# A third sum of g taken by accumulating DMAs in 7 of 25 blocks, with g stored by token halves and the steps from block 8 on in another order

## The chip, the cores and the metric

The kernel runs on one core of one Trainium2 chip. A core has a matrix engine (TensorE, PE in the profile), a vector engine (VectorE, DVE), a scalar engine (ScalarE, ACT), GpSimd (POOL), a queue engine (SyncE, SP) and 16 DMA engines which all queues share. PE reads its operands from on-chip memory and writes into the accumulation memory (PSUM); DVE and ACT read and write both; a DMA can't reach PSUM. Every engine works through its own instruction list in order and waits on semaphores for the others.

The metric is the device time of one execution in microseconds (us). The times of the kernel before are 685.28, 685.20 and 685.03 us, median 685.2.

## The reference

An attention over channels, followed by a feed-forward layer with a tanh-GELU. All inputs are float32.

```python
# q, k, v: (4, 6080, 256); w_in: (256, 2048); w_out: (2048, 256)
qn = q / (norm(q, axis=1) + 1e-6)
kn = k / (norm(k, axis=1) + 1e-6)
s = kn.transpose(0, 2, 1) @ qn / tau          # (4, 256, 256)
a = softmax(s, axis=-1)
x = (v @ a).reshape(24320, 256)
h = x @ w_in
g = 0.5 * h * (1 + tanh(c * (h + 0.044715 * h**3)))
out = g @ w_out                               # (24320, 256)
```

## The kernel before

**The stages.** For each of the four batches the kernel loads q and k as bfloat16, forms their 256x256 product (`gram_row`), the column norms and the softmax, and multiplies the result into the first weight, so that `aw` = a·w_in (256x2048) stands ready for the batch. After that h is `aw` applied to v, and no x is ever formed. This preparation for batch b+1 is spread among the steps of batch b; in the last batch there is none left to spread.

**The blocks.** The tokens are cut into 25 blocks: five of 1024 and one of 960 in each of the first three batches (blocks 0 to 17), five of 1024, one of 512 and one of 448 in the last (blocks 18 to 24). In a block v arrives twice transposed: `lv` issues a casting DMA from POOL into a DRAM buffer (`cast_v`), and `lt` a transposing DMA from SP into `vT` (`load_vt`).

**The first product** makes h with d_ff on the partitions, 16 chunks of 128 by the tokens of the block. Some chunks are computed plainly (`plain`, words `g.`, and `plain_gelu`, words `G.`). The others go in pairs, one chunk of the lower half of d_ff and one of the upper, by a Strassen-Winograd scheme with seven products instead of eight (`small`, words `m1` to `m7`, and `set_step`, words `wcq`, `wy5`, `wap`, `wax`, and the GELUs `wGq`, `wGr`, `wGx`). The GELUs are ACT's and write g as bfloat16 into two tiles for each block, `g_half(n, f)`, where f is the half of d_ff. A tile is `[128, 8, tokens]`: chunk by chunk, with all tokens of the block behind each other.

**The second product** is the same scheme on g: d_ff is cut in two (f = 0, 1), the tokens are cut in two (t = 0, 1), and the output channels are cut in two. Writing g_ft for a quarter of g, DVE forms four sums of quarters in `token_sum` (words `T1` to `T4`, line 704, each in two parts h = 0, 1 of four chunks, that is 128 x 2048 elements in a 1024-token block):

```
T1 = g01 - g00     T2 = g11 - T1     T3 = g11 - g01 (written over g01)     T4 = g10 - T2
```

`product` (line 708; words `M1` to `M7`) then runs four matmuls for each part: M1, M2 and M3 take g00, g10 and g11 into the accumulator `r`; M5, M6, M7 and M4 take T1, T2, T3 and T4 into the accumulator `p`. So T3.h is read by M7.h alone, and M7 is the product whose line reads `p<-g,wcomb` in the profile, since T3 lies in a g tile. The weights for it, with the sums S1 to S4 of quarters of w_out, are built once by `prep_wout` at line 662. `mm2_step` (line 761) combines the accumulators and transposes the results out of them (`c11`, `c12`, `c21`, `c22`), and SP stores them. The last block multiplies directly (`direct`, words `D`).

**The order.** The whole program after the first batch's preparation is one string `ORDER` (line 948) of 3,498 words, such as `T3.0:18` (T3, part 0, block 18) or `m1.2@a:19` (in PSUM bank a). `run` (line 874) takes them one by one, and each puts its instructions at the end of its engine's list. So this string fixes the order on every engine, and that of the DMAs on POOL and SP too. A word stands about where its step is to start: PE's words between two others tell how much matmul work lies between them.

Of the kernel before, what the change touches and what calls it, by code (L numbers as in the profile page):

```python
# [16 lines left out]
def kernel(  # L17
# [493 lines left out]
    def plain_gelu(n, u):  # L511
        t = BLOCKS[n][2]
        hc = t // 2
        hp = PR.pop((n, u))
        if t > 512:
            nc.scalar.activation(g_half(n, u // 8)[:, u % 8].rearrange("p (t x) -> p t x", t=2),  # L516
                                 hp[:, :, :hc], AF.Gelu_apprx_tanh)
        else:
            nc.scalar.activation(g_half(n, u // 4)[:, u % 4 * 2 : u % 4 * 2 + 2, :], hp[:, :, :t],
                                 AF.Gelu_apprx_tanh)  # L520
# [13 lines left out]
    def half_gelu(n, p, t):  # L534
        hc = hc_of(n)
        nc.scalar.activation(g_half(n, p // 4)[:, p % 4 * 2 : p % 4 * 2 + 2, t * hc : t * hc + hc],
                             PR.pop((n, p, t))[:, :, :hc], AF.Gelu_apprx_tanh)
# [69 lines left out]
    def set_step(n, i, what):  # L607
# [54 lines left out]
    def prep_wout(what):  # L662
        if what == "pA11":
            nc.vector.tensor_copy(wc(A11), w_half(0, 0))
        if what == "pF0":
            WF.append(yout.tile([128, 32, 32], FP32, tag="ot", name="wf0"))
            nc.vector.tensor_add(WF[0], w_half(1, 0), w_half(1, 1))
        if what == "pS1":
            nc.vector.tensor_copy(wc(S1), WF[0])
        if what == "pF1":  # L670
            WF.append(yout.tile([128, 32, 32], FP32, tag="ot", name="wf1"))
            nc.vector.tensor_sub(WF[1], WF[0], w_half(0, 0))
# [10 lines left out]
        if what == "pS3":  # L683
            nc.vector.tensor_sub(wc(S3), w_half(0, 0), w_half(1, 0))
# [3 lines left out]
    def quarter(n, f, t, h):  # L688
        hc = hc_of(n)
        return GT[n, f][:, h * 4 : h * 4 + 4, t * hc : t * hc + hc]  # L690

    def token_sum(n, i, h):
# [11 lines left out]
        nc.vector.tensor_sub(o, a, b)  # L704
# [20 lines left out]
    def direct(n, p, t, tag):  # L725

        hc = hc_of(n)
        for m in range(2):
# [218 lines left out]

ORDER = """
# [84 lines left out]
ap:6 sa.2:2 wap.5:7 M7.1:6 T4.1:6 m3.5:7 m7.5:7 M3.0:6 ksq.3:2 wGx.2:7 qsq.3:2 G.4:7 M3.1:6 m1.6@a:7  # L1033
wGq.5:7 f1.3:2 wax.5:7 M7.0:6 m5.6@h:7 m4.5:7 m5.7@b:7 wcq.6:7 c12:6 wy5.6:7 m1.7@r:7 ax:6 m6.6:7
wcq.7:7 M4.0:6 m6.7:7 lq.6:2 lk.6:2 f2.3:2 wGr.5:7 wap.6:7 wy5.7:7 m7.6:7 f3.3:2 wGx.5:7 wap.7:7
m2.6:7 m3.6:7 wax.6:7 M4.1:6 m2.7:7 m7.7:7 c21:6 wGq.6:7 wGx.6:7 wax.7:7 row.3_5@p:2 row.2_4@p:2
m3.7:7 row.3_1@p:2 row.3_2@p:2 row.2_0@p:2 m1.1@s:8 T1.0:7 m4.7:7 wGq.7:7 row.2_5@p:2 m4.6:7 wGx.7:7
row.3_3@p:2 g.8@h:8 vs:8 row.2_2@p:2 row.3_4@p:2 m5.1@b:8 row.3_0@p:2 wGr.6:7 wcq.1:8 sp.3@a:2
row.2_1@p:2 G.8:8 lv.0:10 wy5.1:8 wGr.7:7 m6.1:8 row.2_3@p:2 g.12@h:7 m2.1:8 T1.1:7 wap.1:8 sa.3:2
ksq.4:2 m3.1:8 qsq.4:2 m7.1:8 M5.1@r:7 lv.1:10 M5.0@r:7 m1.2@a:8 wax.1:8 T2.0:7 gc:2 f1.4:2 wGq.1:8  # L1040
G.12:7 m5.2@b:8 m4.1:8 T4.0:7 f2.4:2 wcq.2:8 wy5.2:8 g.0@h:8 wGr.1:8 G.0:8 M1.0@p:7 m6.2:8 m2.2:8
M1.1@p:7 y5:7 g.3@h:8 lt.0:9 lt.1:9 cq:7 wap.2:8 wGx.1:8 f3.4:2 c22:6 sp.4@s:2 sa.4:2 G.3:8 T2.1:7
m3.2:8 M2.1:7 m1.5@s:8 M2.0:7 M6.1:7 m5.5@h:8 wGq.2:8 m7.2:8 lq.7:2 wcq.5:8 T3.0:7 qsq.5:2 T3.1:7
ksq.5:2 wy5.5:8 M6.0:7 m2.5:8 g.11@b:8 m6.5:8 c11:7 wax.2:8 ap:7 f1.5:2 wap.5:8 m4.2:8 G.11:8
wGx.2:8 wGr.2:8 M3.0:7 M3.1:7 f2.5:2 m3.5:8 f3.5:2 wGq.5:8 c12:7 m5.6@b:8 m1.6@a:8 m7.5:8 lk.7:2
M7.1:7 wy5.6:8 sp.5@p:2 M7.0:7 wcq.6:8 qsq.6:2 wax.5:8 T4.1:7 sa.5:2 ax:7 m2.6:8 m4.5:8 m6.6:8
g.4@h:8 row.5_5@p:2 wap.6:8 ksq.6:2 M4.0:7 wGx.5:8 wGr.5:8 m3.6:8 f1.6:2 row.5_4@p:2 row.5_3@p:2
m1.7@s:8 row.4_0@p:2 G.4:8 m7.6:8 m5.7@h:8 row.4_5@p:2 wcq.7:8 wy5.7:8 row.4_2@p:2 m6.7:8 T1.0:8
wax.6:8 wap.7:8 f2.6:2 wGq.6:8 wGx.6:8 row.5_0@p:2 M4.1:7 m2.7:8 c21:7 m7.7:8 m3.7:8 g.12@b:8
wGq.7:8 wax.7:8 row.4_4@p:2 m4.7:8 m4.6:8 f3.6:2 row.4_3@p:2 sp.6@r:2 G.12:8 wGr.6:8 wGr.7:8 T1.1:8  # L1050
g.0@h:9 row.5_2@p:2 row.5_1@p:2 m1.1@a:9 sa.6:2 vs:9 row.4_1@p:2 M5.1@r:8 m5.1@b:9 m1.2@s:9 M5.0@r:8
wGx.7:8 wcq.1:9 gc:2 qsq.7:2 G.0:9 c22:7 M1.1@p:8 wy5.1:9 y5:8 T2.1:8 m6.1:9 wap.1:9 M1.0@p:8
m5.2@h:9 wcq.2:9 cq:8 m2.1:9 m6.2:9 m3.1:9 lv.0:11 m7.1:9 T2.0:8 M2.0:8 M6.0:8 wy5.2:9 wap.2:9
wax.1:9 T3.0:8 m3.2:9 wGq.1:9 ksq.7:2 f1.7:2 wGx.1:9 m4.1:9 wGr.1:9 M2.1:8 m7.2:9 m2.2:9 M6.1:8
m1.3@a:9 wax.2:9 f2.7:2 m5.3@b:9 m4.2:9 c11:8 f3.7:2 ap:8 wGq.2:9 g.8@h:9 wcq.3:9 m6.3:9 wGr.2:9
# [18 lines left out]
m7.6:10 m1.7@r:10 wGq.6:10 wax.6:10 m5.7@b:10 wcq.7:10 wy5.7:10 g.0@h:11 G.0:11 c12:9 m6.7:10
wap.7:10 eT:2 wGx.6:10 m4.6:10 M4.0:9 m2.7:10 m7.7:10 m3.7:10 rsum@a:2 M4.1:9 T1.0:10 g.4@h:11
wax.7:10 m4.7:10 rs:2 c21:9 wGr.6:10 wGq.7:10 aw.0@p:2 aw.1@a:2 m1.1@s:11 G.4:11 vs:11 m5.1@b:11
wGr.7:10 wcq.1:11 g.8@h:11 m6.1:11 wy5.1:11 T1.1:10 M5.0@r:10 ac.1:2 wGx.7:10 wap.1:11 ac.0:2
lt.0:12 M5.1@r:10 c22:9 m7.1:11 wax.1:11 m1.2@a:11 aw.4@p:2 G.8:11 m3.1:11 m5.2@h:11 wcq.2:11 ac.4:2
# [202 lines left out]
```

## Time and profile before

| | value |
|---|---|
| median of 3 runs | 685.2 us (685.03 to 685.28) |
| the profiled execution | 685.17 us, of which 683.4 us are the span that the profile shows |
| granted PE clock | 0.998 of full |
| ACT busy | 621.7 us, 91% |
| POOL busy | 74.1 us, 11% |
| DVE, the sums at line 704 with 2048 elements a partition | 160 of about 1.21 us, and 24 of 1.14 us with 1920 |
| DVE, T3 alone in 1024-token blocks | 40 of 1.211 us |
| DMA share by 16 engines, mean | 67% (software-issued 35.3%, SP's 31.4%) |

How to read the profile: busy time is the union of an engine's instructions. A matmul's record runs from its start to its modelled end, and matmuls overlap in the pipeline; the step from one start to the next tells the rate, the record's length does not. "Idle before" is the time for which the engine stood still before the instructions of a group, with what released it. A line `x4` in a timeline is four instructions merged. The "idle" of POOL's DMA issues is no loss in itself: they wait on purpose for a point in PE's list.

### The profile page before, as it was taken

Reading aid. Unit: us, or ns where it says so; the run is one execution under the profiler, and the core shown is the slowest. Engines: PE = TensorE matmul, PEld = TensorE weight load, DVE = VectorE, ACT = ScalarE, POOL = GpSimd, SP = SyncE. Lnnn points to the kernel's source line nnn. Section 1 sums busy time; section 2 is a strip of 40 time slices with the busy share of each in tenths; the row PEclk is TensorE's granted clock in tenths of the full one; section 3 lists DMA queues with packets and bytes.
Section 4 is the critical chain, followed back from the end, with each engine's and each line's share of the span. In section 5 each row is a group of like instructions: output and inputs, shape, how many; then the busy total and the mean of one; then the engine's idle time right before and its main releaser. Section 6 shows DMA issues by size and latency. Waiting matters only on the chain.

```text
span 683.4 us, 10285 instructions
## 1 busy us (share of the span) xinstructions
PE 665.6 (97%) x3585; PEld 337.1 (49%) x3585; DVE 628.5 (92%) x938; ACT 621.7 (91%) x941; POOL 74.1 (11%) x137
## 2 busy tenths in 40 slices
PE   3999999999999999999999999999999999999997
PEld 2854545454445454444444545545444444444566
DVE  4569999999999999989999999999999999999994
ACT  5389999998899999999989999999988999999983
POOL 4322111011001111010010011101000000000001
PEclk9999999999999999999999999999999999999999
DMA  9998988694677795646467977657275336534415
GB/s 240 208 248 142 160 153 136 106 150 76 120 131 113 134 167 88 108 69 114 85 107 123 178 124 133 104 81 122 43 112 78 48 63 103 85 71 91 76 32 90
DMA packets 161508, 78.80 MB, mean 115 GB/s; under 512 B 148512, under 2 KB 152224, under 8 KB 160736
## 3 DMA queue, kind: packets, MB, share of 16 engines
q0 software_dynamic: 14480, 39.72, 35.3%
q1 hardware_dynamic: 145728, 37.14, 31.4%
q10 hardware_dynamic: 1248, 1.28, 0.6%
q8 instruction: 28, 0.46, 0.3%
q14 instruction: 24, 0.20, 0.1%
HBM read 78.91 MB, written 36.57 MB: 169 GB/s over the span
## 4 chain that ended last, share of the span: by engine, by line
PE 94%; DMA 4%; DVE 0%; ACT 0%; issue 0%; POOL 0%; DVEq 0%; ACTq 0%; POOLq 0%
PE p L482 24%; PE r L482 18%; PE rb L482 17%; PE qp L482 13%; PE h L482 12%; PE G L205 5%; DMA qk_g1b<-in_k_dram 3%; PE e L482 2%; PE awp L374 2%; DMA qk_g1a<-in_q_dram 1%; PE o L482 1%; PE ss L186 0%; PE ss L263 0%; ACT qp L613 0%; PE rk L317 0%
## 5 line engine op out<-in xcount | busy, mean ns | idle before, releaser
L482 PEld LDWEIGHTS <-wcomb 128*128 128x128 bf16 x1408 | 136.6, 98 | 144.5 <-issue 1.3
L482 PE MATMUL p<-t,wcomb 128*128 128x512 bf16 (+2 forms) x576 | 142.5, 373 | 0.0
L482 PE MATMUL r<-g,wcomb 128*128 128x512 bf16 (+2 forms) x576 | 141.7, 373 | 0.0
L626 ACT ACTIVATE g<-qp 128x1024 bf16<-128x1024 f32 (+1 forms) x130 | 132.5, 1023 | 4.4 <-PE qp L482 4.1
L482 PEld LDWEIGHTS <-aw 128*128 128x128 bf16 x872 | 84.7, 98 | 91.3 <-DVE aw L416 1.3
L704 DVE TENSOR_TENSOR t<-g,t 128x2048 bf16<-128x2048 bf16 (+2 forms) x96 | 112.9, 1183 | 0.0
L482 PE MATMUL rb<-tv,sw 128*128 128x512 bf16 (+3 forms) x288 | 100.1, 366 | 0.5 <-ACT qp L613 0.3
L618 DVE TENSOR_TENSOR qp<-rb,yw 128x512 f32<-128x512 f32 (+2 forms) x137 | 93.4, 686 | 7.5 <-ACT yw L616 4.0
L621 DVE TENSOR_TENSOR xw<-rb,yw 128x512 f32<-128x512 f32 (+2 forms) x137 | 92.3, 677 | 5.3 <-PE rb L482 3.8
L516 ACT ACTIVATE g<-h 128x1024 bf16<-128x1024 f32 (+1 forms) x92 | 94.2, 1031 | 2.4 <-PE h L482 2.4
L482 PE MATMUL h<-vT,aw 128*128 128x512 bf16 (+2 forms) x376 | 94.4, 377 | 0.0
L613 ACT ACTIVATE qp<-rb 128x512 f32<-128x512 f32 (+2 forms) x137 | 81.0, 596 | 7.5 <-PE rb L482 5.6
L616 ACT ACTIVATE yw<-qp 128x512 f32<-128x512 f32 (+2 forms) x137 | 81.2, 599 | 5.6 <-PE qp L482 4.2
L482 PEld LDWEIGHTS <-sw 128*128 128x128 bf16 x576 | 56.1, 98 | 56.4 <-issue 1.8
L637 ACT ACTIVATE g<-xw 128x512 bf16<-128x512 f32 (+1 forms) x130 | 82.3, 636 | 0.8 <-DVE xw L621 0.6
L637 ACT ACTIVATE g<-rb 128x512 bf16<-128x512 f32 (+1 forms) x130 | 77.8, 604 | 2.6 <-PE rb L482 2.2
L442 POOL DMA_DIRECT2D vb<-in_v_dram x45 | 22.5, 500 | 338.8 <-PE rb L482 172.2
L704 DVE TENSOR_TENSOR t<-g 128x2048 bf16<-128x2048 bf16 (+2 forms) x48 | 56.7, 1183 | 0.2
L704 DVE TENSOR_TENSOR g<-g,g 128x2048 bf16<-128x2048 bf16 (+2 forms) x48 | 56.6, 1181 | 0.0
L482 PE MATMUL qp<-vT,sw 128*128 128x512 bf16 (+3 forms) x144 | 51.4, 366 | 0.0
L482 PE MATMUL rb<-vT,aw 128*128 128x512 bf16 (+3 forms) x144 | 51.1, 366 | 0.0
L482 PE MATMUL rb<-tv,aw 128*128 128x512 bf16 (+3 forms) x144 | 51.0, 366 | 0.0
(145 smaller groups left out, 816.0 us busy)
## 6 DMA issues: line engine op xcount, KB each, us to landing
out_dram<-ot SPq DMA_DIRECT2D x160, 128.0 KB, 3.0
vb<-in_v_dram POOLq DMA_DIRECT2D x38, 256.0 KB, 4.2
k<-in_k_dram POOLq DMA_DIRECT2D x21, 384.0 KB, 5.4
q<-in_q_dram POOLq DMA_DIRECT2D x21, 384.0 KB, 4.7
out_dram<-ot SPq DMA_DIRECT2D x24, 120.0 KB, 3.0
wst<-in_moe_w_out_dram POOLq DMA_DIRECT2D x2, 1024.0 KB, 11.2
vb<-in_v_dram POOLq DMA_DIRECT2D x6, 240.0 KB, 4.0
qk_f<-in_k_dram ACTq DMA_DIRECT2D x2, 512.0 KB, 7.2
```

The source lines that it names most:

```text
L205: nc.tensor.matmul(G[b][:, jc, :], lhsT=qt[:np_, r, jc * 128 : jc * 128 + 128], rhs=kt[:np_, r, :], start=first and jc == 0, stop=jc == 1, ...
L374: nc.tensor.matmul(ps, lhsT=ET[b][:, jc, ic * 128 : ic * 128 + 128], rhs=win_bf[:, jc, fs * 512 : fs * 512 + 512], start=jc == 0, stop=jc ...
L442: after(nc.gpsimd.dma_start(out=vb[: y - x, :], in_=v[b, t0 + x : t0 + y, :]), gate)
L482: GATE[0] = nc.tensor.matmul(*a, skip_group_check=True, **kw)
L516: nc.scalar.activation(g_half(n, u // 8)[:, u % 8].rearrange("p (t x) -> p t x", t=2), hp[:, :, :hc], AF.Gelu_apprx_tanh)
L613: apart(n, i, 0, "act", nc.scalar.activation(QP[n, i][:, 0, :w], RB[n, i][:, :w], AF.Copy))
L616: apart(n, i, 1, "act", nc.scalar.activation(YW[n, i][:, :w], QP[n, i][:, 1, :w], AF.Copy))
L618: apart(n, i, 1, "dve", nc.vector.tensor_add(QP[n, i][:, 1, :w], RB[n, i][:, :w], YW[n, i][:, :w]))
L621: nc.vector.tensor_add(XW[n, i][:, :w], RB[n, i][:, :w], YW.pop((n, i))[:, :w])
L626: nc.scalar.activation(g[:, k0].rearrange("p (t x) -> p t x", t=2), qp[:, :, :hc], AF.Gelu_apprx_tanh)
L637: nc.scalar.activation(g[:, k0, t], x[:, :w], AF.Gelu_apprx_tanh)
L704: nc.vector.tensor_sub(o, a, b)
```

## The change

Five edits:

1. g is stored by token halves: the tile is `[128, 2, 8, tokens/2]` and no longer `[128, 8, tokens]`, so a quarter's part of four chunks is one contiguous run of 4 KB in each partition. All GELU writes and all reads of g follow.
2. The signs of the second product change, so that T3 is a sum: T1 = g01 - g00, T2 = g11 + T1, T3 = g11 + g01, T4 = g10 - T2, with S1, S2 and S3 of w_out negated to match (`pF0`, `pF1`, `pS3`).
3. In blocks 8, 9, 18, 19, 20, 21 and 22 T3 is not DVE's: POOL issues a DMA that reads g11 and adds it onto g01 in place, two of them in a block. The matmuls of M7 wait for its landing.
4. `y5` of the first product can be put on DVE for listed pairs; the list is empty.
5. The words of `ORDER` are the same 3,498, but from the end of block 6's second product on they stand in another order (with stretches in between that are as they were: most of block 11's, and of blocks 14 to 16). Some PSUM banks are exchanged with it.

```diff
     def g_half(n, f):
         if (n, f) not in GT:
-            GT[n, f] = gp.tile([128, 8, BLOCKS[n][2]], BF16, tag=f"g{f}{'ab'[n % 2]}", name=f"g{f}_{n}")
+            GT[n, f] = gp.tile([128, 2, 8, hc_of(n)], BF16, tag=f"g{f}{'ab'[n % 2]}", name=f"g{f}_{n}")
...
         if t > 512:
-            nc.scalar.activation(g_half(n, u // 8)[:, u % 8].rearrange("p (t x) -> p t x", t=2),
-                                 hp[:, :, :hc], AF.Gelu_apprx_tanh)
+            nc.scalar.activation(g_half(n, u // 8)[:, :, u % 8], hp[:, :, :hc], AF.Gelu_apprx_tanh)
...
         if what == "y5":
             YW[n, i] = set_buffer(n, i, "y")
-            apart(n, i, 1, "act", nc.scalar.activation(YW[n, i][:, :w], QP[n, i][:, 1, :w], AF.Copy))
+            if (n, i) in Y5_DVE:
+                apart(n, i, 1, "dve", nc.vector.tensor_copy(YW[n, i][:, :w], QP[n, i][:, 1, :w]))
+            else:
+                apart(n, i, 1, "act", nc.scalar.activation(YW[n, i][:, :w], QP[n, i][:, 1, :w], AF.Copy))
...
-            nc.vector.tensor_add(WF[0], w_half(1, 0), w_half(1, 1))
+            nc.vector.tensor_sub(WF[0], w_half(1, 0), w_half(1, 1))
...
-            nc.vector.tensor_sub(WF[1], WF[0], w_half(0, 0))
+            nc.vector.tensor_sub(WF[1], w_half(0, 0), WF[0])
...
-            nc.vector.tensor_sub(wc(S3), w_half(0, 0), w_half(1, 0))
+            nc.vector.tensor_sub(wc(S3), w_half(1, 0), w_half(0, 0))
...
     def quarter(n, f, t, h):
-        hc = hc_of(n)
-        return GT[n, f][:, h * 4 : h * 4 + 4, t * hc : t * hc + hc]
+        return GT[n, f][:, t, h * 4 : h * 4 + 4]
...
-        a, b = {1: lambda: (quarter(n, 0, 1, h), quarter(n, 0, 0, h)),
-                2: lambda: (quarter(n, 1, 1, h), TS[n, 1, h]),
-                3: lambda: (quarter(n, 1, 1, h), quarter(n, 0, 1, h)),
-                4: lambda: (quarter(n, 1, 0, h), TS[n, 2, h])}[i]()
-        nc.vector.tensor_sub(o, a, b)
+        if i == 3 and n in SUMS_DMA:
+            nc.gpsimd.dma_start(out=o, in_=quarter(n, 1, 1, h), accum_op=ALU.add)
+            return
+        add, a, b = {1: lambda: (0, quarter(n, 0, 1, h), quarter(n, 0, 0, h)),
+                     2: lambda: (1, quarter(n, 1, 1, h), TS[n, 1, h]),
+                     3: lambda: (1, quarter(n, 1, 1, h), quarter(n, 0, 1, h)),
+                     4: lambda: (0, quarter(n, 1, 0, h), TS[n, 2, h])}[i]()
+        (nc.vector.tensor_add if add else nc.vector.tensor_sub)(o, a, b)
...
+SUMS_DMA = {8, 9, 18, 19, 20, 21, 22}
...
+Y5_DVE = {}
...
 ORDER = """
...
-m3.6:19 m7.6:19 T1.0:19 M4.0:18 wy5.7:19 wap.7:19 wax.6:19 wGx.5:19 wGq.6:19 m7.7:19 m3.7:19 m2.7:19
-wGr.5:19 wGq.7:19 g.8@h:20 c21:18 wax.7:19 T3.0:19 m1.1@s:20 m4.6:19 G.8:20 m4.7:19 g.0@b:20
-wGr.6:19 M1.0@p:19 wGr.7:19 vs:20 m1.2@a:20 G.0:20 T1.1:19 lv.0:22 M5.0@r:19 m5.2@h:20 wcq.2:20
...
+c21:18 wGr.6:19 wax.7:19 m3.7:19 wGr.5:19 wGq.7:19 g.8@b:20 m4.7:19 M1.0@r:19 g.0@h:20 T1.0:19
+m1.1@p:20 m1.2@s:20 G.8:20 wGr.7:19 T1.1:19 vs:20 M5.0@a:19 G.0:20 m5.2@b:20 m5.1@h:20 M5.1@a:19
+T3.0:19 wcq.1:20 m6.1:20 wcq.2:20 m6.2:20 wy5.1:20 wy5.2:20 wap.1:20 M1.1@r:19 wap.2:20 m7.1:20
```

More of the change, by code (lines that the diff above doesn't have):

```diff
@@ L1038 @@
[L1038 to L1055, printed above, removed]
@@ L1074 @@
[L1074 to L1078, printed above, removed]
-T2.1:10 wy5.2:11 m6.2:11 m4.1:11 wGr.1:11 y5:10 m2.1:11 wGq.1:11 wap.2:11 lv.0:13 M1.0@p:10
@@ new lines @@
+G.12:7 f1.4:2 m7.1:8 row.3_0@a:2 m3.1:8 m5.2@b:8 M5.0@s:7 wcq.2:8 wax.1:8 wGq.1:8 m4.1:8 f2.4:2
+m6.2:8 g.0@h:8 wy5.2:8 wGr.1:8 f3.4:2 wap.2:8 wGx.1:8 lt.1:9 G.0:8 row.2_4@a:2 sp.4@p:2 sa.4:2
+row.2_3@a:2 m7.2:8 ksq.5:2 y5:7 m3.2:8 T2.0:7 gc:2 M1.0@p:7 M1.1@p:7 cq:7 lv.1:10 m1.5@a:8 m2.2:8
+g.3@h:8 lt.0:9 wax.2:8 wGq.2:8 m4.2:8 M2.0:7 T2.1:7 T3.0:7 m5.5@b:8 M2.1:7 c22:6 T3.1:7 G.3:8
+g.11@h:8 c11:7 wcq.5:8 qsq.5:2 wy5.5:8 M6.1:7 m6.5:8 G.11:8 M6.0:7 f1.5:2 m2.5:8 wGr.2:8 wGx.2:8
+wap.5:8 ap:7 f2.5:2 lq.7:2 m5.6@h:8 m3.5:8 m7.5:8 wax.5:8 m1.6@r:8 T4.0:7 f3.5:2 wGq.5:8 wcq.6:8
@@ new lines @@
+M3.1:7 m4.5:8 M7.1:7 wGr.5:8 M7.0:7 wy5.6:8 m6.6:8 m5.7@b:8 m2.6:8 sp.5@a:2 T4.1:7 wy5.7:8 wGx.5:8
+wap.6:8 sa.5:2 M3.0:7 m1.7@a:8 m3.6:8 ax:7 wcq.7:8 lv.0:11 qsq.6:2 m7.6:8 M4.1:7 ksq.6:2 c12:7
+m6.7:8 M4.0:7 wax.6:8 wap.7:8 m2.7:8 wGq.6:8 row.5_2@p:2 m7.7:8 m3.7:8 g.4@h:8 row.4_4@p:2
+row.5_0@p:2 wGx.6:8 m4.6:8 c21:7 f1.6:2 wGq.7:8 lk.7:2 G.4:8 wax.7:8 wGr.6:8 f2.6:2 T1.0:8 m4.7:8
+g.12@b:8 g.0@h:9 row.4_3@p:2 row.5_1@p:2 wGr.7:8 G.12:8 row.4_5@p:2 m1.1@s:9 row.4_2@p:2 m1.2@r:9
+row.5_3@p:2 G.0:9 f3.6:2 vs:9 sp.6@a:2 m5.1@b:9 wcq.1:9 m6.1:9 row.5_4@p:2 T1.1:8 m5.2@h:9 wcq.2:9
@@ new lines @@
+g.4@b:14 m2.6:14 sa.5:3 wap.6:14 ax:13 m1.7@s:14 lv.1:16 m3.6:14 row.4_2@p:3 m7.6:14 M4.1:13
+row.4_4@p:3 G.4:14 T4.0:13 M4.0:13 f1.6:3 wax.6:14 m5.7@b:14 wcq.7:14 wGq.6:14 m6.7:14 wy5.7:14
+g.12@h:14 c21:13 wap.7:14 row.5_1@p:3 m4.6:14 row.4_3@p:3 m7.7:14 f2.6:3 lk.7:3 wGx.6:14 m2.7:14
+m3.7:14 G.12:14 wGr.6:14 wGq.7:14 c22:13 wax.7:14 T1.0:14 f3.6:3 g.0@h:15 m1.1@r:15 m4.7:14
+row.4_1@p:3 row.4_5@p:3 wGx.7:14 G.0:15 row.5_2@p:3 g.8@b:15 vs:15 wGr.7:14 M1.1@a:14 row.5_3@p:3
+lt.0:16 row.4_0@p:3 m5.1@h:15 sp.6@s:3 wcq.1:15 T1.1:14 m6.1:15 row.5_5@p:3 m2.1:15 G.8:15
```

373 lines of the change are left out of this document (189 added, 184 removed).

## The prediction

> **What bounds the kernel now.** I read the page first, then busy time in windows of 25 us, then the timeline around T3 and M7, and last the DMA issues.
>
> ```profile
> span 683.4 us, 10285 instructions
> ...
> PE 665.6 (97%) x3585; PEld 337.1 (49%) x3585; DVE 628.5 (92%) x938; ACT 621.7 (91%) x941; POOL 74.1 (11%) x137
> ...
> PE   3999999999999999999999999999999999999997
> ```
>
> PE is full in all slices but the first and the last. The windows show it beside the two engines that feed it (columns: the window, its length, busy time and instructions of each engine, PE's clock, DMA share, GB/s):
>
> ```profile
> 500.00:525.00 25.00, 25.00 (x121) 11.55 (x119) 24.47 (x38) 21.01 (x35) 0.98 (x2) 1.00 0.51 76
> 525.00:550.00 25.00, 24.77 (x118) 11.33 (x116) 23.87 (x35) 24.46 (x41) 0.49 (x1) 1.00 0.54 81
> 550.00:575.00 25.00, 25.00 (x118) 11.31 (x116) 24.57 (x34) 24.79 (x42) 0.49 (x1) 1.00 0.45 78
> ```
>
> 525 to 550 is the only window between 125 us and 675 us in which PE's busy time isn't the whole. DVE and ACT are nearly full too (23.9 to 24.6 and 21.0 to 24.8 of 25), so three engines run side by side; PE ends last. Busy time alone doesn't prove that, since matmul records overlap, so I look at the steps. Four matmuls of 512 columns that take 1.03 us with a last record of 0.38 step by (1.03 - 0.38) / 3 = 0.217 us, and that step is the same wherever such lines stand. Taking each matmul's step in the trace against the usual one for its columns (0.216 us for 512, 0.202 for 480, 0.109 for 256, 0.096 for 224), the excess from 220 us, where the new order begins, to the last matmul at 678.0 us is 1.8 us in all. Some 1.0 us of it are eleven gaps of about 0.1 us, most of them beside 64-row or short matmuls, whose weight load isn't covered; about 0.8 us are waits, most at 525 to 527 us:
>
> ```profile
> 527.07 0.38 PE L482 MATMUL rb<-tv,sw 128*128 128x512 bf16 x1 [0.23 <-DVE qp L618]
> ```
>
> The Trainium skill (Trainium Kernel Development and Optimization, Performance Expectations) calls matmul busy time a bad metric because matmuls are pipelined. By that rule the 97% could hide much waiting and the 17 us below could be worth something; the steps say that it hides 1.8 us.
>
> **The change part by part.**
>
> *DVE's T3 goes.* 14 sums of 1.211 us (line 704, `g<-g,g` with 2048 elements), 17.0 us of DVE. What it saves on PE is at most the waits above: 0.8 us if all were DVE's, 1.8 us if every excess went. Of ACT's work nothing is moved, since the list for `y5` is empty, and ACT has 24.5 to 24.8 of 25 us in blocks 18 and 19. I take 0.4 us, half the waits.
>
> *The accumulating DMA comes.* Trace lines of block 18 show what T3 and M7 do now:
>
> ```profile
> 548.41 1.22 DVE L704 TENSOR_TENSOR g<-g,g 128x2048 bf16<-128x2048 bf16 x1
> ...
> 554.35 1.22 DVE L704 TENSOR_TENSOR g<-g,g 128x2048 bf16<-128x2048 bf16 x1
> ...
> 561.10 1.03 PE L482 MATMUL p<-g,wcomb 128*128 128x512 bf16 x4
> ...
> 562.62 1.02 PE L482 MATMUL p<-g,wcomb 128*128 128x512 bf16 x4
> ```
>
> T3.0 starts 14.2 us ahead of M7.0 (562.62), T3.1 6.75 us ahead of M7.1 (561.10). In the old order 70 and 24 matmuls stand between these words, at 0.216 us 15.1 and 5.2 us; so the list tells the room to within some 1.6 us. In the new order the room from T3's word to M7's, matmuls counted with their steps, is for parts 0 and 1: block 8 12.6 and 12.6 us, 9 23.3 and 13.6, 18 15.5 and 8.8, 19 12.5 and 7.8, 20 17.7 and 12.5, 21 13.4 and 9.3, 22 10.6 and 7.3. The DMA must issue, run and land in that.
>
> No accumulating DMA is in this trace. The nearest rows:
>
> ```profile
> vb<-in_v_dram POOLq DMA_DIRECT2D x38, 256.0 KB, 4.2
> k<-in_k_dram POOLq DMA_DIRECT2D x21, 384.0 KB, 5.4
> q<-in_q_dram POOLq DMA_DIRECT2D x21, 384.0 KB, 4.7
> ...
> wst<-in_moe_w_out_dram POOLq DMA_DIRECT2D x2, 1024.0 KB, 11.2
> ...
> qk_g1b<-in_k_dram POOLq DMA_DIRECT2D x1, 512.0 KB, 17.2
> ```
>
> Sizes are what is written. `vb` reads 512 and writes 256 KB, 768 in all, in 4.2 us; q and k 1152 KB in 5.05 us on average; T3's DMA reads 512 + 512 and writes 512, 1536 KB. The line through the first two gives 5.05 + 0.85 = 5.9 us; towards `wst` (2048 KB, 11.2 us, at the start with the DMA engines full) it is 5.05 + 384/896 x 6.15 = 7.7 us. Lower bound 4.2 us, since it moves twice `vb`'s bytes; upper bound 17.2 us, a load of as many bytes behind others at a DMA share about 1 (0.40 to 0.61 in the windows where T3 runs). An addition that costs more than its bytes would lie in between, and no row tells. I take 6.5 us, near the q and k rows: below all 14 rooms, so no wait. With more the lack is paid on PE in full, since nothing covers it: per block the larger lack of its parts. At 8 us 0.2 + 0.7 = 0.9 us (blocks 19 and 22), at 9 us 3.1, at 10 us 1.2 + 2.2 + 0.7 + 2.7 = 6.8, at 12 us 14.8.
>
> The Trainium skill (DMA: Bandwidth & Descriptors, Anatomy of one DMA) fits a POOL-issued DMA as 2.0 us and bytes over 436 GB/s; my estimate by it, counting the 1 MB that is read, is 4.4 us. The sum would be the same and the late landing below less likely; `vb`, half as many bytes read, measures 4.2 us here.
>
> *What else queues.* POOL issues 14 more DMAs at 0.5 us (`vb` row, 500 ns), 7 us on an engine that is 11% busy. Behind T3's wait for ACT and DVE stand the `lv` of blocks 11, 12 and 21 to 24 and batch 3's first q and k loads. In the new order 10.6 us (block 24) or more lie between `lv` and `lt`, against 3.8 to 4.2 us to landing; between `lt` and the block's first matmul at least 9.3 us in the blocks concerned, against 4.0 to 4.8 us for a transposing DMA. So 0, hidden behind PE's previous block; a transfer twice as slow would just show.
>
> *g by halves and the signs.* GELUs that already write two strided pieces (line 536) take 1025 ns, whole rows (line 516) 1038; DVE's strided sums 1213 ns, contiguous ones (line 243) 1226. 13 ns on some 220 GELUs bound it to 2.9 us of ACT over the whole run, either way; I take 0. Subtracting for adding is the same instruction.
>
> *The new order.* The same 3,498 steps and the same matmuls less one of 32 columns (it cleared a PSUM bank's width), 0.03 us. In it as in the old one many steps stand closely behind what they need. I take as many new waits as old ones vanish, 0.4 us; bounds 0 and, from the densest stretch of the old order after 50 us (1.4 us of excess over 50 to 220 us) laid over the 340 us or so that stand in a new order, twice as long, 3 us. At the end the last GELU (`wGx.3:24`) stands three `D` steps before the last instead of eleven; two of these (2 x 4 x 0.096 = 0.77 us) cover its 0.575 us. 0, at most 0.5 us.
>
> **The sum.** 685.17 us of the profiled execution (683.4 span + 1.8 around it) - 0.4 - 0.03 + 0.4 + 0 = 685.1 us; the median is 0.03 above that execution, so 685.2 us. The own range of this case is 684.0 to 686.6.
>
> **The rivals.**
>
> *The DMA lands late* (slower). Mechanism: M7's matmuls are at the head of PE's list and wait for the DMA's semaphore, first M7.1 of blocks 22 and 19, then of 21 and 18. It decides from about 8.2 us on (0.4 + 0.9 us). For it: small rooms, the 11.2 and 17.2 us rows, transposing DMAs beside it (SP's queue takes 31.4% of the engines), an addition of unknown rate. Against: q and k at 4.7 and 5.4 us. At 10 us: 685.2 + 6.8 = 692.0 us.
>
> *The new order waits on ACT* (slower). ACT is as full as before, and every step now stands elsewhere; at the 3 us bound 685.2 + 3 - 0.4 = 687.8 us. Against: the old order, as tight, loses 0.8 us to waits in 458 us.
>
> *The DMAs crowd out the others.* Transposes or v loads land late and PE has no vT. The stores took 2.8 us at a share about 0.5 and 3.7 in 330 to 520 us, where it is higher; to matter, transposes would have to reach 9 us. A block's lack of 2 us in two blocks: 689 us.
>
> *DVE was what held PE.* Then all excess goes: 685.2 - 1.8 = 683.4 us. Against: PE's steps leave no more, and ACT stays full.
>
> **How the numbers follow.** I call 0.2% (1.4 us) what can be told from no change. Forecast 0.53; late landing 0.25; order 0.12; crowding 0.04; DVE 0.06. Faster has the last case, 0.06; the same 0.53 plus 0.02 of the order and late cases that stay small; slower the rest, 0.39. The likeliest is 685.2 us; the range runs from 683.8 us, near the DVE case, to 692.5 us, just beyond a landing time of 10 us.
>
> **What would show it.** Right: PE's busy time 25 of 25 in nearly every window from 220 us on; T3's DMA landing in 5 to 8 us; no wait of `p<-g` on a DMA; DVE's busy time near 611 us with PE's steps unchanged. Wrong: `p<-g` waiting for a DMA onto `g` in blocks 18 to 22 (late landing); PE waiting for `qp`, `rb` or `g` of ACT and DVE in several places (order); waits of the first matmuls of a block for `vT` (crowding); a last matmul before 676.5 us (DVE).

## The result: slower by 0.25%, and the profile after

| | before | after |
|---|---|---|
| median | 685.23 us (684.84 to 687.07, 10 runs) | 687.18 us (686.27 to 688.00, 10 runs) |
| ratio after/before | | 1.0025, 95% interval 1.0015 to 1.0035 |
| profiled execution | 685.17 us, span 683.4 | 686.68 us, span 684.8 |
| start of the last matmul | 678.03 us | 679.39 us |
| PE's excess over its steps, 220 us to the end | 1.8 us | 3.2 us |

The change costs 1.7 us by the ratio and 1.5 us between the two profiled executions; PE's excess accounts for 1.4 of these. The page of after (busy time, then the row of T3's DMAs: KB written by each, median us to landing):

```profile
span 684.8 us, 10307 instructions
...
PE 666.8 (97%) x3584; PEld 336.6 (49%) x3584; DVE 614.0 (90%) x924; ACT 620.5 (91%) x941; POOL 86.5 (13%) x151
...
g<-g POOLq DMA_DIRECT2D x14, 512.0 KB, 6.1
```

DVE has 14 instructions and 14.5 us less to do, ACT as much as before, and the new DMAs land in 6.1 us. The wait of 525 to 527 us is gone too. But the windows show that PE now misses time elsewhere (columns as before: busy time of PE, PE's weight loads, DVE, ACT, POOL):

```profile
270.00:280.00 10.00, 9.91 (x61) 5.44 (x60) 9.33 (x15) 10.00 (x15) 2.50 (x4) 1.00 0.75 113
280.00:290.00 10.00, 9.95 (x48) 4.48 (x47) 9.02 (x14) 10.00 (x17) 0.88 (x1) 1.00 0.81 153
...
590.00:600.00 10.00, 9.85 (x46) 4.25 (x45) 8.99 (x13) 10.00 (x18) 1.77 (x2) 1.00 0.51 90
```

The same windows of the kernel before:

```profile
270.00:280.00 10.00, 10.00 (x63) 5.73 (x62) 9.70 (x17) 9.08 (x14) 0.00 (x0) 1.00 0.43 74
280.00:290.00 10.00, 10.00 (x50) 4.56 (x49) 9.64 (x14) 9.91 (x17) 0.51 (x1) 1.00 0.81 132
...
590.00:600.00 10.00, 10.00 (x48) 4.54 (x47) 9.93 (x14) 9.99 (x17) 0.49 (x1) 1.00 0.62 104
```

Read DVE and ACT together: in these three windows DVE has 0.7 to 1.0 us to spare after the change and ACT has none. A full ACT alone doesn't explain the loss, since in two of the windows ACT was as full before, and PE lost nothing. The timeline at the first of these places, 278 to 280 us (start, duration, engine, line, operation; in brackets the idle time before it and its releaser):

```profile
276.01 1.98 ACT L516 ACTIVATE g<-h 128x1024 bf16<-128x1024 f32 x2
...
277.82 1.15 ACT L613 ACTIVATE qp<-rb 128x512 f32<-128x512 f32 x2
...
278.06 0.38 PE L482 MATMUL qp<-tv,sw 128*128 128x512 bf16 x1
278.53 0.38 PE L482 MATMUL rb<-tv,sw 128*128 128x512 bf16 x1
...
278.81 0.67 ACT L619 ACTIVATE yw<-qp 128x512 f32<-128x512 f32 x1
...
279.51 0.70 DVE L621 TENSOR_TENSOR qp<-rb,yw 128x512 f32<-128x512 f32 x1 [0.60 <-ACT yw L619]
...
280.26 0.38 PE L482 MATMUL qp<-vT,sw 128*128 128x512 bf16 x1
```

ACT works without a gap: two GELUs, two copies for `cq`, one for `y5`. The matmul at 278.53 (`m6` of block 9) needs the first copy, begun only at 277.82; the one before it began at 278.06, so the step is 0.47 us in place of 0.216: 0.25 us are lost. DVE then stands idle for 0.60 us until ACT's `y5` copy is done, and its sum comes too late for the matmul at 280.26, which loses another 0.21 us. DVE was relieved of T3, and here it waits for ACT.

None of these losses is in the profile's table of PE's waits, which is empty for after from 220 us on: a wait shorter than a matmul's record (0.38 us) hides in it. They show only as steps that are too long. There are ten steps that are too long by 0.1 us or more after 220 us, 1.9 us in all; they begin at 278.06, 279.94, 286.33, 303.95, 309.69, 310.29, 532.15, 585.56, 595.70 and 642.37 us; before had four, 0.76 us. The longest new one (0.31 us) ends at 596.22:

```profile
594.94 1.23 DVE L708 TENSOR_TENSOR t<-g 128x2048 bf16<-128x2048 bf16 x1 [0.44 <-ACT g L629]
...
596.22 0.33 PEld L482 LDWEIGHTS <-wcomb 128*128 128x128 bf16 x3 [0.64 <-DVE t L708]
```

DVE stood idle for 0.44 us ahead of T1, for ACT's GELU, then PE waited for T1. Of the 1.9 us, 0.59 us (three steps) end directly with ACT, 0.52 us (at 279.94 and 595.70) with a DVE step that had itself waited for ACT, and 0.80 us (five steps) with DVE steps ahead of which DVE had no idle time. Of the 14 DMAs of T3, 12 landed within 7.9 us. The two of block 18 didn't, and that has a story of its own:

```profile
547.13 2.75 SPq L447 DMA_TRANSPOSE vT<-vb  x2
548.63 0.93 POOL L702 DMA_DIRECT2D g<-g  x1 [7.20 <-DVE tv L558]
553.35 0.86 POOL L702 DMA_DIRECT2D g<-g  x1 [3.80 <-ACT g L639]
561.61 1.03 PE L482 MATMUL p<-g,wcomb 128*128 128x512 bf16 x4
563.55 1.03 PE L482 MATMUL p<-g,wcomb 128*128 128x512 bf16 x4
```

They took 10.6 and 9.3 us from issue to landing. The second lands at 562.7 and M7.1 reads it at 563.55 (0.9 us to spare), so PE didn't wait in this execution. The first was issued 1.5 us after one transposing DMA and at the same moment as the next, which itself took 10.7 us to land; the other 44 transposing DMAs of this execution took 3.0 to 8.1.

### The profile page after: what moved, and what is told of

The parts are those of the page before. It is cut to its first block, busy times and chain, and to the rows that moved or that the text cites. A ratio compares the mean times of both kernels' runs of the same rounds, so it can differ in the third digit from the quotient of the medians.

```text
span 684.8 us, 10307 instructions
## 1 busy us (share of the span) xinstructions
PE 666.8 (97%) x3584; PEld 336.6 (49%) x3584; DVE 614.0 (90%) x924; ACT 620.5 (91%) x941; POOL 86.5 (13%) x151
## 4 chain that ended last, share of the span: by engine, by line
PE 91%; DMA 4%; ACT 3%; issue 1%; DVE 1%; POOL 0%; DVEq 0%; ACTq 0%; POOLq 0%
PE p L482 23%; PE r L482 18%; PE rb L482 17%; PE qp L482 12%; PE h L482 11%; PE G L205 5%; DMA qk_g1b<-in_k_dram 3%; PE e L482 2%; PE awp L374 2%; DMA qk_g1a<-in_q_dram 1%; PE o L482 1%; ACT g L639 1%; ACT g L629 1%; ACT g L516 0%; ACT qp L613 0%
## 5 line engine op out<-in xcount | busy, mean ns | idle before, releaser
L482 PE MATMUL qp<-vT,aw 128*128 128x512 bf16 (+3 forms) x144 | 50.5, 366 | 0.0
```

Source lines behind the costliest of these rows:

```text
L482: GATE[0] = nc.tensor.matmul(*a, skip_group_check=True, **kw)
```

## The experiments

All kernels start from the changed one, so "old order" means its layout and signs with the old `ORDER`. PE's excess is computed as in the prediction, from 220 us on and split at 375 us. Traces of the experiments lack single matmul records here and there (a gap of just one more step); those are left out, and where a lacking record lies inside a wait, its step is taken off the wait. The time between the same two matmuls in a run and in the kernel with the same order gives the same excess to 0.1 us. Runs of all kernels, of the one before too, scatter by 2 us and single ones by up to 5, and some profiles show one reason: the first matmuls of a block at 86 us, ahead of every change of the order, wait 0 to 2.6 us for `vT`.

| run | ratio to before (95% interval) | excess 220 to 375, later (us) |
|---|---|---|
| before, after | 1, 1.0025 (1.0015 to 1.0035) | 0.4, 1.4; 1.5, 1.7 |
| e1 old order, T3 on DVE | 1.0006 (0.9993 to 1.0018) | 0.4, 1.4 |
| e2 new order, no T3 in the seven blocks | 1.0015 (1.0007 to 1.0024) | 1.5, 1.7 |
| e3 new order in the first half alone | 1.0018 (1.0006 to 1.0030) | 1.5, 1.4 |
| e4 new order in the second half alone | 1.0015 (1.0003 to 1.0028) | 0.4, 2.7 |
| e5 new order, T3 on DVE | 1.0190 (1.0170 to 1.0210) | 5.5, 9.9 |
| e6 old order, 14 DMAs | 1.0220 (1.0183 to 1.0258) | one wait of 12.4 |
| e7 14 copies from ACT to DVE | 1.0093 (1.0073 to 1.0112) | 3.9, 7.7 |
| e8 eight words of PE moved | 1.0042 (1.0027 to 1.0057) | 2.2, 3.3 |
| e9 block 18's DMA, word moved | 1.0042 (1.0024 to 1.0060) | block 18: 2.7 |
| e10 old order, 10 DMAs | 1.0000 (0.9987 to 1.0013) | 0.4, 1.4 |
| e11 old order, block 16's DMAs alone | 1.0179 (1.0161 to 1.0197) | one wait of 12.1 |
| e12 as e11, one word moved | 1.0206 (1.0172 to 1.0240) | one wait of 9.3 |
| e13 as e11, DMA held back | 1.0002 (0.9994 to 1.0011) | 0.4, 1.4 |
| e14 after, block 18's DMA held back | 1.0026 (1.0016 to 1.0035) | 1.5, 1.7 |
| e15 as e11, transposing DMAs held back | 0.9998 (0.9988 to 1.0009) | 0.4, 1.4 |
| e16 old order, 14 DMAs, one held back | 1.0017 (1.0008 to 1.0026) | 0.4, 2.4 |
| e17 after, four words of PE moved | 1.0019 (1.0010 to 1.0028) | 1.3, 1.7 |

### Which part of the change costs (e1 to e4)

e1 takes the layout and the signs alone; e2 takes the new order and leaves the third sums of the seven blocks out altogether (neither DVE nor a DMA makes them, M7 reads g01 as it is).

```diff
 # e1
-SUMS_DMA = {8, 9, 18, 19, 20, 21, 22}
+SUMS_DMA = {}
-ORDER = """ (new)
+ORDER = """ (old)
 # e2
+        if i == 3 and n in {8, 9, 18, 19, 20, 21, 22}:
+            return
 # e3: new order up to the middle of block 14, old from there, DMAs in blocks 8 and 9
 # e4: old order up to the middle of block 14, new from there, DMAs in blocks 18 to 22
```

> g by token halves and the changed signs alone, in the old order, T3 on DVE in every block. If the storage of g costs (ACT's GELUs write two pieces for one), the time is some of the 1.7 us above the kernel before: 686 us or more, and line 516 or 629 is longer by over 10 ns. If the order or the DMAs cost, this is 685.2 +- 0.3 us with ACT's rows unchanged. I expect the latter.

> The changed kernel without T3 in blocks 8, 9 and 18 to 22: neither DMA nor DVE forms it, and M7 takes g01 as it is. DVE and the order are as in the changed kernel, the 14 DMAs are gone. If the new order's chains of ACT and DVE steps cost the time, 687 us stays (686.3 to 687.3) and the waits at 278, 280, 310 and 596 us are still there. If the DMAs cost it, by landing late or by slowing what runs beside them, it falls to 685.4 us or less. In between, both.

> The new order for blocks 7 to 13 with the DMAs of blocks 8 and 9, the old order (banks renamed) from the middle of block 14 on with T3 on DVE. The profile shows 1.1 us of new PE excess in 220 to 330 us and hardly any net excess behind it. If the order costs where it shows, this kernel carries most of the loss: 686.2 us. If the late DMAs of the last blocks cost it, 685.2 us.

> The old order up to the middle of block 14, the new one behind it with the DMAs of blocks 18 to 22. By the profile's excess (1.3 us against 1.25 us from 475 us on) this is level with the kernel before, 685.2 +- 0.4 us. If the slow landings of block 18's DMAs (10.6 and 9.3 us in the profile, M7 0.9 us behind) are what other executions wait for, it is 686 to 687 us with a wider spread than the kernel before.

e1 is the same as before: 685.87 us, and its profile has the old waits in place (104 ns at 520.7, 150 ns at 524.6, about 0.4 us at 526.2, where one matmul record is lacking). From 220 us to the last matmul it takes as long as the kernel before to within 0.05 us. So the layout of g and the signs cost nothing that can be measured. (Of the sums of w_out only S3 is negated; in S1 and S2 the code changes the sign of some of the terms. The steps are as many and of the same kind.)

e2 is as slow as after within the intervals (686.67 us), though there is no third sum on any engine. Its waits are those of after, to within 2 ns: 254 ns at 278.75, 210 at 280.63, 149 at 287.02, 148 at 304.64, 185 at 532.85, 156 at 586.27, 313 at 596.40. From 220 us to the last matmul it takes as long as after to within 0.02 us. The same two instructions in its timeline, with the same idle times:

```profile
280.20 0.70 DVE L621 TENSOR_TENSOR qp<-rb,yw 128x512 f32<-128x512 f32 x1 [0.60 <-ACT yw L619]
```

```profile
595.64 1.23 DVE L710 TENSOR_TENSOR t<-g 128x2048 bf16<-128x2048 bf16 x1 [0.44 <-ACT g L629]
```

So it is the order, and not the DMAs, that costs; leaving out all 14 sums doesn't buy the waits back. The order includes the exchanged PSUM banks; e3, whose second half is the old order with banks renamed, has there the excess of before (1.4 us), so renaming alone cost nothing in that half.

e3 and e4 each showed a loss of their own. By PE's excess the first half holds most of it: 1.5 us in place of 0.4, at 277 to 311 us. In the second half the new order removes the waits of 521 to 527 us (0.65 us) and adds 1.0; of e4's 2.7 us, 0.74 are M7.1 of block 18 waiting for a DMA that took 10.9 us. That is the side of late landings that I had named for e4, and its runs spread from 685.42 to 690.50 us. That e4 (median 686.86 us) is as slow as e3 (687.11 us) is not wholly accounted for.

### Who is late in the new order (e5, e7, e8, e17)

```diff
 # e5: after with T3 on DVE
-SUMS_DMA = {8, 9, 18, 19, 20, 21, 22}
+SUMS_DMA = {}
 # e7: after with 14 of ACT's y5 copies on DVE
-Y5_DVE = {}
+Y5_DVE = {(8, 6), (8, 7), (9, 1), (9, 2), (9, 3), (10, 1), (10, 2), (18, 3), (20, 4), (20, 5), (20, 6), (20, 7), (22, 6), (22, 7)}
```

The words that e8 moves, each to just before the second one of its pair (e17 moves the four of the first line alone):

```
row.5_4 m6.1:9   row.4_0 m3.1:9   row.7_0 m4.7:9   m2.3:10 m3.2:10
M5.1:8 m3.1:9    M6.1:8 M2.1:8    m5.5:20 m4.4:20  m5.2:21 M5.1:20
```

> The changed kernel, but all 14 third sums back on DVE (17 us of DVE work), no accumulating DMA; order, layout and signs of after. If the new order's waits are of ACT alone, the step excess of PE from 220 us on stays near 3.2 us and the time near 687. If the DMAs buy the new order something, DVE's sums bring new waits and PE's excess rises, to 4 us or more, and the time to 688 or more. If the DMAs cost something that the earlier run without third sums did not show, this one is faster than after, 686 or less.

> The changed kernel with 14 copies (y5, 0.62 us each, line 619) moved from ACT to DVE, ahead of the places where PE waits: blocks 8, 9, 10, 18, 20 and 22. The results stay the same. If ACT's chain is what the new order waits on: the waits near 278, 280, 286, 532 and 596 us vanish or shrink, PE's excess falls from 3.2 to 2.2 us or less, time 685.5 to 686.4. If it is DVE or the order of PE alone: the waits stay or grow, 687 or more.

> The changed kernel with eight matmul words moved up by a few places, so that PE has other matmuls to do at six of its new waits (278, 280, 286, 304, 310, 585 and 596 us); nothing else is moved. If these waits are what the change costs: about 1.2 us of PE's excess goes, the last matmul comes 1.0 to 1.3 us earlier, time 685.6 to 686.3. If the time is lost elsewhere, or the waits only move on to the next step: excess near 3 us, 687.

> The changed kernel with four matmul words moved up by one or two places, ahead of the waiting step at 278, 280, 304 and 310 us. If a filled wait is time won: PE's excess over its steps from 220 us on falls from 3.2-3.6 us to 2.7-3.0 and the time to 686.3 to 686.9. If the waits only move on to the next step behind ACT and DVE: excess and time as before, 3.2 us or more, 687.0 to 687.6.

With T3 back on DVE the new order takes 698.91 us, 12 us more than with the DMAs. Its table of PE's waits, empty for after, names DVE first (waited for, total us, times, longest):

```profile
PE rb L482 <- DVE xw L624: 3.2, 4, 1.0
PE rb L482 <- DVE qp L621: 2.4, 3, 0.9
PE qp L482 <- DVE qp L621: 1.8, 2, 1.3
```

The timeline shows one of them, from T3 on:

```profile
284.95 1.22 DVE L708 TENSOR_TENSOR g<-g,g 128x2048 bf16<-128x2048 bf16 x1
...
286.08 1.22 DVE L708 TENSOR_TENSOR t<-g,t 128x2048 bf16<-128x2048 bf16 x1
...
287.22 0.69 DVE L624 TENSOR_TENSOR xw<-rb,yw 128x512 f32<-128x512 f32 x1
...
287.96 0.38 PE L482 MATMUL rb<-tv,aw 128*128 128x512 bf16 x1 [1.03 <-DVE xw L624]
```

The sum for which PE waits (word `wax`) stands behind T3 and T2 on DVE. In the new order T3's word stands more matmuls ahead of M7 than in the old in 11 of the 14 parts, as a DMA needs; on DVE that can put it ahead of steps which PE needs sooner, as here. The DMAs are worth 12 us to this order, and it has used them up.

e7 missed its forecast: 692.68 us. 4.0 us of its excess are M7 of block 18, whose DMAs took 15.2 and 14.2 us (below). The rest, some 4.4 us over after, came with the copies, which are the only edit. PE got new waits for DVE; just ahead of the first of them DVE makes a copy, and PE waits until DVE has caught up:

```profile
268.99 0.69 DVE L617 COPY yw<-qp 128x512 f32<-128x512 f32 x1
...
270.39 0.38 PE L482 MATMUL rb<-vT,aw 128*128 128x512 bf16 x1 [0.69 <-DVE sv L193]
```

So a relief of ACT can't be bought from DVE in this order; the run doesn't show what relief of ACT alone would bring, and no run does.

e8 missed as well (688.82 us). Three of its eight words were moved ahead of what they need themselves: `m5.2:21` waited 0.95 us for DVE's sums of v, `m4.1:9` 0.58 us behind the `M5.1:8` put before it, `M6.1:8` 0.15 us; another 0.95 us are M7 of block 18. It tells only how tight the list is. e17 moves four words up by a few places. The waits at 278 (254 ns), 304 (147) and 310 us (167 and 159) are gone, and that at 280 falls from 212 to 163 ns, 0.78 us in all; but that at 286 us grows from 149 to 362 ns, and the rest came back in smaller steps. From 220 us to the last matmul e17 is 0.15 us quicker than after (excess 3.0 against 3.2 us), so most of what was filled came back later. The time, 686.39 us, is 0.8 us below after, but the intervals overlap: between "won" and "moved on" this isn't settled by the time, and by the steps it is mostly moved on.

### What the DMA costs by itself (e6, e10)

```diff
 # e6: old order; T3's words moved up to where their inputs are ready (room to M7 9.9 us or more)
-SUMS_DMA = {8, 9, 18, 19, 20, 21, 22}
+SUMS_DMA = {8, 9, 15, 16, 17, 19, 20}
 # e10: the same, fewer blocks
+SUMS_DMA = {8, 9, 17, 19, 20}
```

> Old order, layout and signs of after, and 14 third sums by accumulating DMA in blocks 8, 9, 15, 16, 17, 19 and 20, whose words alone are moved up to where their inputs are ready (9.9 us or more of matmuls ahead of M7). Nothing else of the order is changed. If the order and not the DMA costs the time: not slower than before, the 0.5 us of waits at 525 to 527 us shorter or gone, 684.7 to 685.4. If the DMAs themselves cost (by slowing ACT, crowding loads or landing late): 686 or more, with p<-g waiting or waits spread over the seven blocks.

> Old order with ten third sums by accumulating DMA, in blocks 8, 9, 17, 19 and 20, words moved up; blocks 15 and 16 are back on DVE, the rest as in the run that took 702. If the 17 us of that run were the collision in block 16 alone: 685.0 to 685.8, no wait of p<-g, though one DMA of block 20 may land late into its room of 12.7 us. If the DMAs cost something wherever they are under the old order: 687 or more.

e6 fell on the other side than I expected: 702.18 us (695.95 to 706.55). But not all over: 11 of its DMAs landed in 4.7 to 8.3 us, one in 10.6 into a room that held it, and the two of block 16 in 16.6 and 22.3 us. M7 of block 16 waited for them, and PE stood still for 12.4 us:

```profile
514.00:516.00 2.00, 0.00 (x0) 0.00 (x0) 0.00 (x0) 0.00 (x0) 0.00 (x0) 0.50 1.44 180
516.00:518.00 2.00, 0.00 (x0) 0.00 (x0) 0.00 (x0) 0.00 (x0) 0.00 (x0) 0.50 1.17 86
...
524.00:526.00 2.00, 2.00 (x6) 0.76 (x5) 0.00 (x0) 0.00 (x0) 0.00 (x0) 0.50 0.07 16
```

All four engines are idle in the first two windows, the DMA engines move data, and the granted clock has fallen to 0.50 (the number after POOL's). It is still 0.50 after PE has restarted at 523.35 us, and the steps there take 0.2 us longer for some 4 us. Without blocks 15 and 16 (e10) the time is that of before, 685.62 us: ten sums off DVE by DMA, nothing gained, nothing lost.

### Why some land late (e9, e11 to e16)

```diff
 # e11: old order, DMAs in block 16 alone, T3's words as in e6;   e12: its first T3 word moved beside the second
+SUMS_DMA = {16}
 # e9: after; T3.0:18 moved behind M1.1:18
 # e13, e14, e16: as e12, e9 and e6, and the moved DMA waits for the last matmul ahead of its word
-            nc.gpsimd.dma_start(out=o, in_=quarter(n, 1, 1, h), accum_op=ALU.add)
+            after(nc.gpsimd.dma_start(out=o, in_=quarter(n, 1, 1, h), accum_op=ALU.add),
+                  GATE[0] if (n, h) in GATED else None)
 # e15: as e11; lt.0:18 and lt.1:18 some 10 us later in the list, and waiting for a matmul there
-        nc.sync.dma_start_transpose(out=vt_tile(n)[:, :, x:y], in_=v_bf.pop((n, h))[: y - x, :])
+        after(nc.sync.dma_start_transpose(out=vt_tile(n)[:, :, x:y], in_=v_bf.pop((n, h))[: y - x, :]),
+              GATE[0] if n == 18 else None)
```

> The changed kernel with one word moved: the accumulating DMA of block 18's first part some 2 to 3 us later, so that it isn't issued at the same moment as a transposing DMA (at 548.6 us both were, and landed after 10.6 us). If that coincidence makes both late: the two DMAs of block 18 land within 8 us, no wait of p<-g near 563 us, and the time falls to that of the new order without third sums, 686.3 to 686.8. If long landings come of something else, landings stay at 9 to 12 us and the time at 687.0 to 687.6.

> Old order, third sums by DMA in block 16 alone, words where the run of 702 had them (beside the transposing DMAs of block 18). If the collision is what cost: landings of 15 us and more, a wait of p<-g of 8 to 13 us near 511 us, time 693 to 702. If it took the many DMAs together: landings below 8 us, 685.0 to 685.8.

> As the run before it, with one word moved: the first of the two DMAs issues beside the second, 4 to 5 us after the transposing DMAs. If the coincidence of issue makes them late: both land within 9 us, rooms 12.7 and 10.3 us, no wait, 685.0 to 685.8. If block 16's DMAs are late wherever they are: 690 or more.

e11 shows the loss with a single block: 697.89 us. e9 and e12 tried to part the two kinds of DMA by moving a word, and didn't part them: T3.0 was issued at 549.01 us in e9 and at 495.77 in e12, again within 0.05 us of a transposing DMA. In both, POOL stood at this DMA until its semaphores were met, and issued it then, though the word stood further back. Both runs were as slow as their unmoved counterparts or slower. A dependence on a matmul does hold the DMA back:

> Old order, third sums by DMA in block 16 alone, the first of them made to wait for a matmul some 4 us later, so that it really issues 4 to 5 us after the transposing DMAs. If issue beside a transposing DMA makes both late: the two land within 9 us, the transposing ones within 8, no wait of p<-g, 685.0 to 685.8. If something else of this stretch (v loads, stores) does it: landings of 12 us and more, 690 or more.

> The changed kernel with the first DMA of block 18 made to wait for a matmul that ends some 2.5 us later than it issued. If it is the coincidence with the transposing DMA that delays them: both land within 8 us, p<-g waits nowhere, and the time falls by the 0.5 us that stood between after and the order without third sums: 686.2 to 686.9. If not: landings of 9 us and more, 687 or more.

> Old order, third sums by DMA in block 16 alone, as in the run of 698, but the two transposing DMAs of block 18 made to wait some 10 us instead. If the two kinds disturb each other: the accumulating DMAs land within 8 us, no long wait of p<-g, 685.0 to 686.2. If the accumulating DMAs are late by themselves here: still 17 us and more, 693 or more.

> Old order and all 14 DMAs of the run that took 702 (blocks 8, 9, 15, 16, 17, 19, 20), the first of block 16 held back as above. If that one collision was the 17 us: 685.0 to 686.5, with landings up to 11 us in block 20 that its room hides. If the sum of many DMAs costs: 688 or more.

The timeline, and the DMA table (KB of each, median us to landing) of 493 to 512 us, first for e11, where the two are issued together:

```profile
497.13 5.24 SPq L447 DMA_TRANSPOSE vT<-vb  x2
497.17 0.93 POOL L702 DMA_DIRECT2D g<-g  x1 [0.67 <-DVE tv L558]
501.74 0.87 POOL L702 DMA_DIRECT2D g<-g  x1 [3.65 <-ACT g L639]
523.78 1.89 PE L482 MATMUL p<-g,wcomb 128*128 128x512 bf16 x4 [11.97 <-DMA g<-g]
```

```profile
g<-g POOLq DMA_DIRECT2D x2, 512.0 KB, 20.1
out_dram<-ot SPq DMA_DIRECT2D x6, 128.0 KB, 5.6
vb<-in_v_dram POOLq DMA_DIRECT2D x2, 256.0 KB, 11.6
vT<-vb SPq DMA_TRANSPOSE x2, 20.9
```

and for e13, where the accumulating DMAs wait until 502 (the edit makes them wait for a matmul; the bracket names what ended last by the profile):

```profile
497.15 5.57 SPq L447 DMA_TRANSPOSE vT<-vb  x2
502.04 1.83 POOL L702 DMA_DIRECT2D g<-g  x2 [5.51 <-ACT qp L613]
```

```profile
out_dram<-ot SPq DMA_DIRECT2D x8, 128.0 KB, 5.0
g<-g POOLq DMA_DIRECT2D x2, 512.0 KB, 6.8
vb<-in_v_dram POOLq DMA_DIRECT2D x2, 256.0 KB, 5.7
vT<-vb SPq DMA_TRANSPOSE x2, 5.8
```

The two transposing DMAs start at 497.15 and 501.47 us here, so the first accumulating one comes 4.9 us behind the one and 0.57 us behind the other. Not issued at the same moment, the 20 us become 6 to 7, for both kinds, and the 12 us of PE's wait are gone: 685.46 us. e15 does it from the other side, with the accumulating DMAs at 495.45 and 500.03 and the transposing ones from 505.66 on:

```profile
g<-g POOLq DMA_DIRECT2D x2, 512.0 KB, 7.3
...
vT<-vb SPq DMA_TRANSPOSE x2, 4.6
```

685.27 us. So either kind is quick when the other isn't issued at the same moment, and issued together both are slow. e16 brings the 14 DMAs of e6 from 702.18 down to 686.80 us with block 16 parted. The 1.2 us that it still has over e10 are in the profile one wait of 0.97 us at 470 us, which e6 has too. Its timeline shows a second price of such a DMA:

```profile
467.65 0.92 POOL L702 DMA_DIRECT2D g<-g  x1 [6.78 <-ACT g L629]
468.25 1.39 POOL L294 TENSOR_TENSOR rt<-sv,halves 128x4 f32<-128x4 f32 x1
...
469.68 0.17 DVE L300 TENSOR_SCALAR rt<-rt 128x4 f32<-128x4 f32 x1 [1.08 <-POOL rt L294]
...
470.94 0.38 PE L482 MATMUL rb<-vT,aw 128*128 128x512 bf16 x1 [0.81 <-DVE ot L749]
```

The DMA of block 15 holds POOL's list for 6.8 us until ACT's GELU is done. POOL's own step `rt` stands behind it and starts at 468.25 us; in e10, without a DMA in block 15, it starts at 461.91. DVE then waits 1.08 us for `rt`, and PE for what DVE does next. No run moves this DMA alone.

e14 parts them in the changed kernel. Block 18's DMAs then land in 5.2 and 8.0 us, but the time stays (687.49 us; I had expected 0.5 us less), and so does PE's excess. So block 18 is not what makes the changed kernel slower; the order is.

## Why the prediction was wrong

**The step that failed.** "I take as many new waits as old ones vanish, 0.4 us" (the new order). The old waits of 0.1 us and more did vanish (0.76 us), and more than my half of 0.8; but the new order brought 1.9 us of such waits, 1.1 us of them between 277 and 311 us, where before had 0.1. The excess rose from 1.8 to 3.2 us. The bounds that I had given, 0 to 3 us, held it, and the rival "the new order waits on ACT" described the larger part of what happened: several short waits, of which 0.59 us end with ACT and 0.52 us with a DVE step that had waited for ACT; the other 0.80 us end with DVE alone. It forecast 687.8 us at its bound; 687.2 was measured. I gave it 0.12, because the old order, as tight, loses little. That was no evidence: the old order's fit to these engines says nothing of another order's. The check that I left out was to lay ACT's and DVE's steps in the new order, with their durations from the trace, beside PE's.

**DVE's relief.** I took 0.4 us of gain from it. In the old order e10 and e13 show none (1.0000 and 1.0002, with ten and two sums off DVE). The wait of 526 us, which I put half to DVE, stays in e10 and e13 (0.4 us) though they take sums off DVE in blocks 17 and 16. In the new order it is worth 12 us (e5 against after), but only against waits that this order itself makes; against the kernel before nothing of it is left. The old waits at 521 to 527 us are gone in e5 too, where T3 is on DVE, so it is the order that removed them.

**The DMA's price.** 6.5 us taken, 6.1 measured (4.5 to 10.6), bounds 4.2 and 17.2. That no M7 waits, and so 0 for after, was right for the profiled execution, and e14 agrees for the median. It was close: block 18's second DMA took 9.3 us against a room of 8.8 us by the list, and was in time because it was issued 10.2 us ahead of its M7; in the profiles of e4 and e8 the same M7 waited 0.74 and 0.95 us. At the issue I had taken 0.5 us of POOL; it is 0.87. The Trainium skill (DMA: Bandwidth & Descriptors, Anatomy of one DMA) had given 4.4 us by my estimate; the quickest of the 14 took 4.5, and the traces agree with it as a floor.

**Late landing and crowding** had mechanisms that exist and that I had wrong in cause. I had counted on bytes and a slow addition, and on transposes reaching 9 us. A transposing DMA did take 10.7 us, and e6 and e11 show 12 us of PE's time lost to a late landing; but not for their size, which is the same in quick and slow blocks of 1024 tokens: the slow ones were issued together with a transposing DMA, or came next behind one that was.

**Layout and signs** at 0: right (e1). **The tail** at 0: right, the last matmul comes 1.4 us later and the excess explains that much. **"Wrong" signs:** "PE waiting for `qp`, `rb` or `g` of ACT and DVE in several places (order)" was the one that came true, though the table of waits doesn't show it.

**What stays open:** how much of the new order's loss relief of ACT, or another order of DVE's steps, would bring back. The waits shown go back to ACT, those at 304, 310, 586 and 642 us end with DVE, and e7 doesn't part them.

## What to carry to other kernels

Where another engine is the limit, an engine's relief is worth at most what the limiting one waits for it; here PE waited under 0.8 us for DVE and ACT together, and the reordering that came with the DMAs cost more, while e10 put ten of them into the old order at no cost. Look for losses in the steps from one matmul to the next, since waits shorter than a matmul's record can be missing from the table of waits. Keep an accumulating DMA from being issued at the same moment as a transposing one by a dependence that holds one of them back; in e9 and e12 moving its word alone didn't move its issue. And look at what stands behind such a DMA in its engine's list, since it waits with it.

## What the runs showed of the hardware that I had not expected

Over after and all experiments with such DMAs, 144 accumulating DMAs are on record. Twelve were issued within 0.15 us of a transposing DMA, and all twelve took 10.5 to 18.1 us. Of the other 132, 122 took 4.5 to 8.5 us. Nine of the remaining ten are the second DMA of a block whose first was one of the twelve, 4.6 to 6.1 us behind it, and took 9.1 to 22.3 us; the tenth stood 0.4 us behind a transposing DMA and took 10.2. Why the moment of issue matters so much isn't shown: one issued 0.6 us after a transposing DMA took 6.1 us, and eight issued 0.2 to 0.4 us ahead of one took 5.4 to 6.5. The Trainium skill (DMA: Bandwidth & Descriptors, Rules for kernel authors) says that a transpose beside ordinary DMAs needs nothing; that speaks of results, and for time these runs differ: 20 us in e11 against 6 in e13.

An accumulating DMA keeps POOL for 0.87 us at its issue, where a plain casting load keeps it for 0.50.
